# A convolution and a gated product pair on one core: product 2 begins in tile 0 and follows by 60 steps, unit 1 convolved in the ring, new work lists

## The chip, the cores and the metric

The kernel runs on one core of one Trainium2 chip. The metric is the time of one execution in microseconds (us) as the device measures it. Its engines work side by side, each on its own queue of instructions, and wait for each other by semaphores: TensorE (PE, matrix products), VectorE (DVE), ScalarE (ACT), GpSimd (POOL) and SyncE (SP, which here issues transfers). Product results are written to PSUM, which has eight banks of 512 float32 for each of 128 partitions.

## What is computed

The input x has 8 sequences of 4096 positions with 192 channels. A causal convolution with 7 taps mixes positions; its weights are a softmax over the taps, one set for each of 8 heads of 24 channels. The result, as 32768 rows of 192, goes through a product pair with h cos h between.

```python
w = exp(weight - max(weight)); w = w / (sum(w) + 1e-09)        # 8 heads x 7 taps
c[b, s, head, g] = sum_k w[head, k] * x_padded[b, s + k, head, g]
x = c.reshape(32768, 192)
h = x @ w_in                   # 192 -> 2048
g = h * cos(h)
out = g @ w_out                # 2048 -> 192, float32
```

## The kernel before

The rows are cut into 64 tiles of 512 rows (four blocks of 128); two tiles make a unit, so there are 32 units of 1024 rows. All products are taken in bfloat16 and summed in float32.

A unit passes these stations. Its rows are loaded by SP (`load_unit`, 768 KB, and `load_edges`, 96 KB, for the rows before each block). GpSimd casts them to bfloat16 (`cast_unit`). TensorE convolves them with banded matrices in two parts of four heads each (`conv_part`, part 0 named d or c, part 1 named c, lines 191 and 218). ScalarE copies the two banks of a part to `ct` (`conv_out`, line 200). GpSimd doubles `ct` in its free direction (`double_unit`), so that one transfer on SP's queue can transpose it into `cT` (`turn_unit`, line 263) and each column block is there twice, on rows 0 to 63 and 64 to 127. GpSimd mends the first six positions of each block, which need rows of the block before (`mend_edges`). Unit 0 goes another way: its first half is transposed on TensorE (`conv_first`, `turn_first`), its second half is convolved by `conv_rest` with both band halves, doubled while it is copied out, and transposed by a transfer.

A tile then has eight pairs j of column blocks of w_in. `mm1` (line 387, "h0" to "h7") fills two banks with six matmuls. `gcu` (line 399, "s0" to "s7") lets ScalarE take the cosine (a sine with a bias) and VectorE multiply it with h into `g`. `mm2_step` (line 412, "m5" is five steps) makes product 2: 64 steps a tile, two matmuls each, one on the upper and one on the lower 64 rows of the array, so that they run side by side into two banks, `o_ps0` and `o_ps1`. After step 32 the row halves change banks. `Turn` (line 162) guards such a change: an empty instruction on SP's queue waits for the last matmuls of the first half, and the first ones of the second half wait for it. The half-array parts of a convolution use it as well. "q" marks the middle of a tile's product 2 and "p" its end. `evac` copies the two banks out, bank 0 on ScalarE ("P") and bank 1 on VectorE ("Q"), and `store` writes 384 KB. The last tile sums its four blocks in four separate banks, and `finish` copies and stores them one by one.

PSUM holds a ring of three tiles of two banks (`h_pool`) for `mm1` and for convolution parts, and the two banks of product 2. A new ring tile can be written only when the one that had its banks has been read.

The order of work is written out by hand. TensorE's is one list a tile, `PE_ORDER`, with `PE_FIRST` for the first four tiles; ScalarE's and VectorE's follow `ACT_ORDER` and `ACT_FIRST` ("er", "ec1", "ed2" are the copies of convolution parts). The loop at line 480 walks TensorE's list and lets ScalarE's go on as far as its entries have been made. Transfers and GpSimd's work are tied to p and q (lines 526 to 555). Product 2 lags: tile 0 has none of it, and in the steady list a tile of `mm1` begins when the product 2 of two tiles earlier still has 21 steps to go, so 85 steps are left between the two. In tiles 0 and 1 convolutions are made with all 128 rows at once (`whole`), in tile 0 into the banks of product 2 (`o_banks`), which are idle there.

At the start, `band` is filled by sixteen small copies shared out by a string, D for VectorE, P for GpSimd, A for ScalarE (line 318); the first matmuls of the convolution (line 337) need them.

Of the kernel before, what the change touches and what calls it, by code (L numbers as in the profile page):

```python
# [16 lines left out]
def kernel(  # L17
# [72 lines left out]

    def cast_wo(q):
        nc.gpsimd.tensor_copy(out=wo[:, q * HP : (q + 1) * HP], in_=wo_f[:, q * HP : (q + 1) * HP])

# [94 lines left out]

    ct_tiles = {}

    def conv_mm(u, c, ps, i, rows, n0, n1, prev=0, **flags):
# [26 lines left out]
    def conv_part(u, c, banks, whole=False):  # L218


        ps = banks()
        nb = UB + (u == 1)
        sides = [slice(0, 64), slice(64, 128)]

        def mm(i, rows, **flags):
            return conv_mm(u, c, ps, i, sides[rows], 0, nb, **{"start": False, "stop": False, **flags})

        if whole:
            for i in range(4):
                conv_mm(u, c, ps, i, slice(0, 128), 0, nb, start=i % 2 == 0, stop=i % 2 == 1)  # L230
            if u == 2 and c == 0:
                spread_taps(ps[1][:, UB * 2 * G : UB * 2 * G + K])
            yield
        else:
            mm(0, 0, start=True)
            mm(2, 1, start=True)
            turn = Turn()
            turn.mark(mm(1, 0), mm(3, 1))
            yield
            turn.wait(mm(2, 0), mm(0, 1))  # L240
            mm(3, 0, stop=True)
            mm(1, 1, stop=True)
        yield
        if c == 0 and u not in ct_tiles:
            ct_tiles[u] = ct_pool.tile([128, UB + 1, NC, 2, 64], BF16, name="ct")
        for b in range(2):
            conv_out(u, c, ps, 0, 0, nb, nc.scalar.copy, banks=(b,))
            if b and u == 2 and c == 0:
                nc.scalar.copy(tap, ps[1][:, UB * 2 * G : UB * 2 * G + K])
            yield  # L250

    cT = {}

    def double_unit(u):

        ct = ct_tiles[u]
        nb = UB + (u == 1)
# [4 lines left out]

    def turn_unit(u, n0=0, n1=UB + 1):
        ct = ct_tiles.pop(u)
        if u not in cT:
# [17 lines left out]
    def mend_edges(u):  # L283

        if u == 1:
            nc.gpsimd.tensor_copy(out=cT[u][:, 0:UB, :, 0 : K - 1],
# [30 lines left out]
    three = {"D": nc.vector.tensor_copy, "A": nc.scalar.copy, "P": nc.gpsimd.tensor_copy}  # L317
    for i, k in enumerate("DPDPDPADPDPADPAD"):
        q, rows = divmod(i, 4)
# [43 lines left out]
    def conv_rest():  # L363
        banks = o_banks()
        for c in range(2):
            for i in range(4):
                for prev in range(2):
                    conv_mm(0, c, [b[:, 4 * G * 2 * c :] for b in banks], i, slice(0, 128), NB + 1 - prev, UB + 1 - prev, prev,
                            start=c == 0 and prev == 0 and i % 2 == 0, stop=c == 1 and prev == 1 and i % 2 == 1)
        yield  # L370
        for b in range(2):
            for c in range(2):
                conv_out(0, c, [x[:, 4 * G * 2 * c :] for x in banks], NB, NB, UB, copies[1 - b], True, (b,))
        yield
# [3 lines left out]
    turn_first(1)  # L378
    cast_unit(1, 0, NB)
    cast_unit(1, NB)  # L380

# [5 lines left out]
    def mm1(t, j, n0=0, n1=NB):  # L387

        c = cT[t // TPU]
        m0 = (t % TPU) * NB  # L390
# [7 lines left out]

    def gcu(t, j, h, n0=0, n1=NB):
        cs = cos_pool.tile([128, 2, T], BF16, name="cs")  # L400
        part = slice(n0 * 128, n1 * 128)
# [7 lines left out]

    STEPS = 2 * NF  # L410

    def mm2_step(q):
# [13 lines left out]
        else:  # L426

            si, f = divmod(k, NF)
            if half == 0 and f == 0:
                for b in range(2):  # L430
                    o_ps[tt, b, si] = (o_pools[b].tile([128, T], FP32, name="o_ps%d" % b) if si else
                                       ring_banks()[0])[:, 0:D]
            first, last = half == 0 and f == 0, half == 1 and f == NF - 1
        ms = []
        for r in range(2):
# [4 lines left out]
                                       rhs=wo[rows, f // 2, f % 2, :], start=first, stop=last, skip_group_check=True))  # L440
        if i == STEPS - 1:
            turns[tt] = Turn()
            turns[tt].mark(*ms)
        if i == STEPS:
            turns.pop(tt).wait(*ms)

    def evac(t, b):
        if t not in o_sb:
            o_sb[t] = opool.tile([128, NB, D], FP32, name="o_sb")
        copies[b](o_sb[t][:, 2 * b : 2 * b + 2, :].rearrange("p s d -> p (s d)"), o_ps.pop((t, b)))  # L450

# [4 lines left out]
    def finish(t):  # L456
        o_sb[t] = opool.tile([128, NB, D], FP32, name="o_sb")
        for si in range(2):
            for b in range(2):
                copies[b](o_sb[t][:, 2 * b + si, :], o_ps.pop((t, b, si)))  # L460
                store(t, 2 * b + si, 2 * b + si + 1, [nc.scalar, nc.sync][b])

    o_ps, o_sb, turns = {}, {}, {}

    PE_ORDER = "h0 m4 c1 m6 c2 m4 h1 m7 h2 p h3 m13 h4 m10 h5 m6 h6 m3 q h7 m11"
    ACT_ORDER = "s0 ec1 Q ec2 s1 P s2 s3 s4 s5 s6 s7"

    PE_FIRST = ["h0a h0b h1 h2 h3 r h4 h5 d1 d2 h6 h7 c1 c2",
                "p h0 m5 h1 m5 h2 m6 h3 m12 h4 m2 h5 m2 q d1 d2 m5 h6 m6 c1 c2 m3 h7 m3",
                "m5 h0 c1 m10 p c2 h1 h2 m7 h3 m2 h4 m14 h5 m5 h6 m4 q h7 m1",
                "m11 h0 m3 c1 m5 c2 m3 h1 m9 p h2 h3 m10 h4 m9 h5 m8 h6 m5 q h7 m11"]
    ACT_FIRST = ["s0a s0b s1 s2 er s3 s4 s5 ed1 ed2 s6 ec1 ec2 s7", "s0 s1 s2 s3 s4 s5 ed1 ed2 s6 ec1 ec2 s7",
                 "s0 P Q ec1 s1 ec2 s2 s3 s4 s5 s6 s7", ACT_ORDER]

    HALVES = {"": (0, NB), "a": (0, NB // 2), "b": (NB // 2, NB)}
    step = 0
    for t in range(NT + 2):  # L480
        u, second = divmod(t, TPU)
        cu, cc = (u + TPU, second) if t >= TPU else (1 + t, 1)
        conv = {"c": conv_part(cu, cc, ring_banks if t else o_banks, t < TPU) if cu < NU else iter(())}
        if t < TPU:
            conv["d"] = conv_part(cu, 0, ring_banks if t else o_banks, True)
        if t == 0:
            conv["r"] = conv_rest()
        act, done, h = (ACT_ORDER if t >= len(ACT_FIRST) else ACT_FIRST[t]).split(), set(), {}

        def flush():  # L490
            while act:
                k = act[0]
                need = {"P": "p", "Q": "p", "e": "r" if k == "er" else k[1:2] + "2"}.get(k[0], "h" + k[1:])
                if need not in done:
                    return
                act.pop(0)
                if k[0] in "PQ":
                    if 0 <= t - 2 < NT - 1:
                        evac(t - 2, "PQ".index(k[0]))
                elif k[0] == "e":  # L500
                    next(conv[k[1]], None)
                    if k == "er":
                        turn_unit(0, NB, UB)
                        load_unit(2)
                        load_edges(2)
                        cast_wo(0)
                elif k[0] == "s" and t < NT:
                    gcu(t, int(k[1]), h.pop(k[1:]), *HALVES[k[2:]])

        for k in (PE_ORDER if t >= len(PE_FIRST) else PE_FIRST[t]).split():  # L510
            if k[0] == "h" and t < NT:
                h[k[1:]] = mm1(t, int(k[1]), *HALVES[k[2:]])
            elif k[0] in conv:
                next(conv[k[0]], None)
            elif k[0] == "m":
                for q in range(step, step + int(k[1:])):
                    mm2_step(q)
                step += int(k[1:])
            elif k[0] == "p":
                assert step % (2 * STEPS) == 0  # L520
            elif k[0] == "q":
                assert step % (2 * STEPS) == STEPS
            done.add(k)
            flush()

            if k == "q":
                if second == 0 and t and u + 1 < NU:
                    mend_edges(u + 1)
                if t == 1:
                    cast_unit(3)  # L530
                    mend_edges(1)
                if second == 0 and u + 3 < NU:
                    cast_unit(u + 3)
            if k == "p":
                if second == 1 and t > 1 and cu < NU:
                    double_unit(cu)
                if second == 0 and t and u + 1 < NU:
                    turn_unit(u + 1)
                if t == 1:
                    turn_unit(1)  # L540
                if 0 <= t - 2 < NT - 1:
                    store(t - 2)
                if t == NT + 1:
                    finish(NT - 1)
            if k == ("p" if t > 1 else "q") and second == 1 and u + 4 < NU:
                load_unit(u + 4)
                load_edges(u + 4)
        if t == 0:
            double_unit(1)
            cast_wo(1)  # L550
            load_unit(3)
            load_edges(3)
            cast_unit(2)
        if t == 1:
            double_unit(2)

# [29 lines left out]
```

## Time and profile before

| What | Value |
|---|---|
| median of 3 runs | 713.9 us (713.43 to 715.75) |
| profiled execution, first to last instruction | 714.0 us |
| TensorE busy, matmuls | 703.3 us, 11828 |
| VectorE, ScalarE, GpSimd busy | 646.7, 590.4, 300.9 us |
| cosine of a pair (L402, 128x1024) | 1028 ns |
| multiply of a pair (L406, 128x1024) | 1222 ns |
| copy of a convolution bank (L209, 128x384; 128x432) | 483 ns; 548 ns |
| copy with doubling (L343, 128x768) on ScalarE | 799 ns |
| copies out of product 2 (L450) on VectorE, ScalarE | 558 ns, 473 ns |
| first product of a tile begins (L395) | 10.44 us |
| last matmul ends | 710.49 us |

An instruction's mean time is from its start to its end; neighbours on one engine overlap a little, so that multiplies in a row start some 1.14 us apart and cosines 0.92. A line L395 is line 395 of the kernel. "PE" is TensorE at a matmul and "PEld" the load of its weights, which runs beside matmuls. "SPq" stands for SP's queue. An arrow such as "<-DVE g L406" names what ended the idle time before an instruction. A granted clock of 1.00 is full speed of TensorE.

### The profile page before, as it was taken

To read this page: it belongs to the slowest core of one execution; us is meant where nothing else is said; L and a number is where in the kernel's file an instruction comes from. 1 tells how busy PE (TensorE), PEld (TensorE's weight loads), DVE (VectorE), ACT (ScalarE), POOL (GpSimd) and SP (SyncE) were. 2 spreads that over 40 slices of the span, in tenths; PEclk is the share of its full clock that TensorE was granted. 3 is DMA by queue.
4 is the path that set the end of the run, shared out by engine and by line. 5 is a ranking of instruction groups with operands and counts; after the bars stand their busy time and mean duration, and the time that the engine had idled before them with its cause. 6 is when DMAs were issued, how large, how long until landed. Compare 5 with 4: busy or idle time off the path is not lost.

```text
span 714.0 us, 26519 instructions
## 1 busy us (share of the span) xinstructions
PE 703.3 (99%) x11828; PEld 538.3 (75%) x11829; DVE 646.7 (91%) x601; ACT 590.4 (83%) x719; POOL 300.9 (42%) x307
## 2 busy tenths in 40 slices
PE   7899999999999999999999999999999999999997
PEld 3577777777777777777777777777777777777776
DVE  7799999999999999999999999999999999999995
ACT  7788888888888888888888888888888888888774
POOL 6553345553245533445543355534355533453200
PEclk9999999999999999999999999999999999999999
DMA  8954553545644535544546534445535565513402
GB/s 213 232 110 115 145 127 100 138 94 127 146 104 115 142 86 137 146 107 113 126 94 146 144 97 124 113 107 145 137 91 138 98 122 145 122 52 92 95 25 68
DMA packets 183713, 85.25 MB, mean 119 GB/s; under 512 B 111664, under 2 KB 183216, under 8 KB 183600
## 3 DMA queue, kind: packets, MB, share of 16 engines
q1 hardware_dynamic: 182888, 82.59, 48.3%
q8 instruction: 92, 1.51, 0.9%
q0 software_dynamic: 416, 0.79, 0.8%
q14 instruction: 21, 0.17, 0.1%
q10 hardware_dynamic: 296, 0.20, 0.1%
HBM read 31.36 MB, written 25.17 MB: 79 GB/s over the span
## 4 chain that ended last, share of the span: by engine, by line
PE 96%; DVE 1%; DMA 1%; ACT 1%; issue 0%; POOL 0%; POOLq 0%; SPq 0%
PE o_ps L439 47%; PE h L395 46%; PE h L194 3%; DMA cT<-ct 1%; DVE g L406 0%; ACT cs L402 0%; PE h L439 0%; DVE band L320 0%; POOL mask L131 0%; ACT mask L136 0%; ACT ct L343 0%; PE o_ps L194 0%; DVE diag L309 0%; DVE cT L361 0%; PE h L358 0%
## 5 line engine op out<-in xcount | busy, mean ns | idle before, releaser
L406 DVE TENSOR_TENSOR g<-h,cs 128x1024 bf16<-128x1024 f32 (+1 forms) x513 | 606.4, 1220 | 32.3 <-ACT cs L402 21.8
L402 ACT ACTIVATE cs<-h 128x1024 bf16<-128x1024 f32 (+1 forms) x513 | 511.9, 1026 | 102.2 <-PE h L395 68.2
L439 PEld LDWEIGHTS <-g 64*128 64x128 bf16 x8192 | 369.5, 94 | 91.2 <-issue 1.2
L439 PE MATMUL o_ps<-wo,g 64*128 64x192 bf16 x8128 | 434.9, 243 | 0.0
L395 PE MATMUL h<-cT,w 64*128 64x512 bf16 (+1 forms) x3078 | 413.7, 376 | 4.7 <-DVE g L406 2.5
L395 PEld LDWEIGHTS <-w 64*128 64x128 bf16 x3078 | 161.1, 94 | 72.4 <-issue 4.8
L292 POOL TENSOR_TENSOR edge_prod<-cT,tap 128x1008 f32<-128x1008 bf16 x30 | 67.2, 2239 | 347.0 <-DMA cT<-ct 347.0
L183 POOL CAST x_bf<-x_f 128x1728 bf16<-128x1728 f32 (+2 forms) x33 | 80.6, 2444 | 6.7 <-DMA x_f<-in_x_dram 6.7
L209 ACT CAST ct<-h 128x384 bf16<-128x384 f32 x120 | 51.8, 483 | 8.5 <-PE h L194 4.8
L450 DVE COPY o_sb<-o_ps 128x384 f32<-128x384 f32 x63 | 35.2, 558 | 23.6 <-PE o_ps L439 23.2
L258 POOL COPY ct<-ct 128x1536 bf16<-128x1536 bf16 (+1 forms) x31 | 45.6, 1472 | 3.4 <-ACT ct L209 3.4
L194 PE MATMUL h<-x_bf,band 64*128 64x192 bf16 (+1 forms) x472 | 41.0, 243 | 0.0
L297 POOL TENSOR_TENSOR edge_prod<-edge_prod 128x144 f32<-128x144 f32 x60 | 33.3, 554 | 4.7
L295 POOL TENSOR_TENSOR edge_prod<-edge_prod 128x432 f32<-128x432 f32 x30 | 30.3, 1009 | 2.4
L450 ACT COPY o_sb<-o_ps 128x384 f32<-128x384 f32 x63 | 29.8, 473 | 1.6 <-PE o_ps L439 1.6
L194 PEld LDWEIGHTS <-band 64*128 64x128 bf16 (+1 forms) x496 | 24.7, 94 | 2.1 <-issue 1.0
L298 POOL TENSOR_TENSOR cT<-edge_prod 128x144 bf16<-128x144 f32 x30 | 18.3, 608 | 2.4
L260 POOL COPY ct<-x_bf 128x192 bf16<-128x192 bf16 x60 | 19.2, 349 | 0.0
L108 PE MATMUL o_ps<-zero 128*128 128x512 bf16 x12 | 4.7, 554 | 1.3 <-DVE zero L103 1.3
L108 PEld LDWEIGHTS <-zero 128*128 128x128 bf16 x15 | 1.6, 121 | 3.3 <-issue 1.9
L460 DVE COPY o_sb<-h 128x192 f32<-128x192 f32 x1 | 0.4, 358 | 3.7 <-PE h L439 3.7
L460 ACT COPY o_sb<-h 128x192 f32<-128x192 f32 x1 | 0.3, 319 | 3.8 <-PE h L439 3.8
(62 smaller groups left out, 43.3 us busy)
## 6 DMA issues: line engine op xcount, KB each, us to landing
out_dram<-o_sb SPq DMA_DIRECT2D x63, 384.0 KB
x_f<-in_x_dram SPq DMA_DIRECT2D x30, 768.0 KB
x_f<-in_x_dram SPq DMA_DIRECT2D x31, 96.0 KB
x_f<-in_x_dram SPq DMA_DIRECT2D x4, 384.0 KB
wo_f<-in_moe_w_out_dram SPq DMA_DIRECT2D x4, 384.0 KB
w<-in_moe_w_in_dram POOLq DMA_DIRECT2D x2, 384.0 KB, 6.3
cT<-ct SPq DMA_TRANSPOSE x32
out_dram<-o_sb ACTq DMA_DIRECT2D x2, 96.0 KB
```

The costliest lines, as they stand in the source:

```text
L183: copy(out=bf[u][:, n0 + o : n1 + o, :].rearrange("p n (h k r) -> p (n h) k r", k=NC, r=R), in_=x_tiles[u][:, n0:n1, :].rearrange("p n (h ...
L194: return nc.tensor.matmul(out=ps[i // 2][:, 0 : (n1 - n0) * 2 * G].rearrange("p (n k i r) -> p i n k r", n=n1 - n0, k=NC, i=2)[:, i % 2], ...
L209: copy(o[:, :, 0, :], i[:, :, 0, :])
L258: nc.gpsimd.tensor_copy(out=ct[:, 0:nb, :, 1, :], in_=ct[:, 0:nb, :, 0, :])
L292: nc.gpsimd.tensor_tensor(out=edge_prod, in0=window, in1=tap.rearrange("p (a b k) -> p a b k", a=1, b=1).to_broadcast([128, NC * UB, K - 1 ...
L295: nc.gpsimd.tensor_tensor(out=edge_prod[:, :, :, 0:3], in0=edge_prod[:, :, :, 0:3], in1=edge_prod[:, :, :, 3:6], op=ALU.add)
L297: nc.gpsimd.tensor_tensor(out=edge_prod[:, :, :, 0], in0=edge_prod[:, :, :, 0], in1=edge_prod[:, :, :, j], op=ALU.add)
L395: nc.tensor.matmul(out=h[:, i, n0 * 128 : n1 * 128], lhsT=w[rows, k, j, :], rhs=c[rows, m0 + n0 : m0 + n1, k, :], start=(k == 0), stop=(k ...
L402: nc.scalar.activation(out=cs[:, :, part], in_=h[:, :, part], func=AF.Sin, bias=math.pi / 2.0, scale=1.0)
L406: nc.vector.tensor_tensor(out=g_tiles[t][:, 2 * j : 2 * j + 2, part], in0=h[:, :, part], in1=cs[:, :, part], op=ALU.mult)
L439: ms.append(nc.tensor.matmul(out=o_ps[tt, b, si], lhsT=g_tiles[tt][rows, f, s * 128 : (s + 1) * 128], rhs=wo[rows, f // 2, f % 2, :], star ...
L450: copies[b](o_sb[t][:, 2 * b : 2 * b + 2, :].rearrange("p s d -> p (s d)"), o_ps.pop((t, b)))
```

## The change

The lists are written anew, and GpSimd's work and the transfers, which were tied to p and q, become entries of TensorE's list: K casts a unit, L loads one, D doubles, X transposes, Y mends, W casts half of w_out, O stores what is ready; a digit names the unit where it is not that of the steady rule. Twelve steps of product 2 stand in tile 0, and 87 are issued by the end of tile 1 (49 before). In the steady list four steps of the last tile's product precede the next tile, which makes the lag 60. Copies out of product 2 follow p in the same tile. X stands after c2 in even tiles, Y in odd ones.

Unit 1 takes ring banks for its convolution in tile 0, since the two other banks are in use. `conv_rest` gives each half of the heads a bank of its own, and ScalarE copies each in one instruction of 128x768. Three more parts (d1, c1 and those of unit 2) are made with 128 rows as before, under names with the unit's number. In the last tile the two groups of blocks go through fourteen of sixteen column blocks each before the last two of each, each group has its own Turn, and bank 1 of the tile before is copied by ScalarE ("A"). ScalarE gives one of its three band copies to GpSimd. The assertions on `have` check the lists while the program is built and leave no instruction. The core of the diff:

```diff
-    for i, k in enumerate("DPDPDPADPDPADPAD"):
+    for i, k in enumerate("DPDPDPDPDPDPDPAA"):
...
+                    h = 4 * c + i
+                    nc.tensor.matmul(out=banks[c][:, 0 : 2 * D].rearrange("p (n k i r) -> p i n k r", n=NB, k=NC, i=4)[:, i],
+                                     lhsT=band[:, h, 128 * prev : 128 * prev + 128],
...
-        for b in range(2):
-            for c in range(2):
-                conv_out(0, c, [x[:, 4 * G * 2 * c :] for x in banks], NB, NB, UB, copies[1 - b], True, (b,))
+        for c in range(2):
+            nc.scalar.copy(
+                out=ct_tiles[0][:, NB:UB, :, :, 4 * R * c : 4 * R * (c + 1)].rearrange("p n k t w -> p (n k) t w"),
+                in_=banks[c][:, 0 : 2 * D].rearrange("p (m t w) -> p m t w", t=1, w=4 * R).to_broadcast(
+                    [128, NB * NC, 2, 4 * R]))
...
-    cast_unit(1, 0, NB)
-    cast_unit(1, NB)
...
+    LAST_HALF = [(si, f) for f0, f1 in ((0, NF - 2), (NF - 2, NF)) for si in range(2) for f in range(f0, f1)]
...
-            si, f = divmod(k, NF)
+            si, f = divmod(k, NF) if half else LAST_HALF[k]
...
-        if i == STEPS - 1:
-            turns[tt] = Turn()
-            turns[tt].mark(*ms)
-        if i == STEPS:
-            turns.pop(tt).wait(*ms)
+        if tt < NT - 1:
+            if i == STEPS - 1:
+                turns[tt] = Turn()
+                turns[tt].mark(*ms)
+            if i == STEPS:
+                turns.pop(tt).wait(*ms)
+        elif f == NF - 1 and half == 0:
+            turns[tt, si] = Turn()
+            turns[tt, si].mark(*ms)
+        elif f == 0 and half == 1:
+            turns.pop((tt, si)).wait(*ms)
...
-    PE_ORDER = "h0 m4 c1 m6 c2 m4 h1 m7 h2 p h3 m13 h4 m10 h5 m6 h6 m3 q h7 m11"
-    ACT_ORDER = "s0 ec1 Q ec2 s1 P s2 s3 s4 s5 s6 s7"
...
+    PE_ORDER = "m11 h0 m4 h1 m6 h2 m7 q Y K h3 m7 h4 m7 c1 m4 c2 X L m5 h5 m9 p h6 D O h7 m4"
+    ACT_ORDER = "s0 s1 s2 s3 s4 ec1 ec2 Q s5 P s6 s7"
...
+    PE_FIRST = ["K1 h0a h0b W0 h1 h2 h3 r h4 d11 h5 d21 W1 c11 X0 m1 h6 m11 h7 L2 c21 D1",
+                "m6 K2 h0 m1 L3 h1 K3 m13 q h2 m3 h3 m9 h4 m6 h5 m3 X1 c12 m11 p c22 h6 d12 h7 L4 L5 m17 c13 m4 c23 m1 d22 Y1 D2 m1",
+                "h0 m2 h1 m7 q K4 h2 m11 h3 X2 O m8 h4 Y2 m13 p h5 h6 m9 h7 m7",
+                "h0 m8 h1 m8 q h2 m7 h3 m7 O m1 h4 m3 d13 m4 d23 m6 h5 m4 p h6 h7 m4 D3"]
+    ACT_FIRST = ["s0a s0b s1 s2 er s3 s4 ed11 ed21 s5 ec11 s6 ec21 s7",
+                "s0 s1 s2 s3 s4 s5 ec12 ec22 Q P s6 ed12 s7 ed22 ec13 ec23",
+                "s0 s1 s2 s3 Q s4 P s5 s6 s7",
+                "s0 s1 s2 s3 s4 ed13 ed23 Q s5 P s6 s7"]
+
+    PE_LAST = "m10 h0 m3 h1 m13 h2 m2 q h3 m10 h4 m3 h5 m7 h6 m12 p h7 O m7"
+    ACT_LAST = "s0 s1 s2 s3 s4 s5 s6 P A s7"
...
+    for v in (1, 2, 3):
+        for i, part in enumerate("dc"):
+            conv[part, v] = conv_part(v, i, ring_banks, v < 3)
...
+        def of_unit(k, v):
+            if (k, v) == ("K", 1):
+                cast_unit(1, 0, NB)
+                cast_unit(1, NB)
+            elif (k, v) == ("X", 0):
+                turn_unit(0, NB, UB)
+            elif k == "L":
+                load_unit(v)
+                load_edges(v)
+            else:
+                {"K": cast_unit, "D": double_unit, "X": turn_unit, "Y": mend_edges}[k](v)
...
+            else:
+                v = {"D": cu, "X": u + 1, "Y": u + 1, "K": u + 3, "L": u + 4}[k]
+                if t >= 2 * TPU and v < NU and (k in "DLY") == bool(second):
+                    of_unit(k, v)
```

## The prediction

> **What bounds the kernel now.** I read the page's busy shares and slices first, then TensorE's timeline, then windows laid on the clock's steps, then the chain of waits.
>
> ```profile
> span 714.0 us, 26519 instructions
> ...
> PE 703.3 (99%) x11828; PEld 538.3 (75%) x11829; DVE 646.7 (91%) x601; ACT 590.4 (83%) x719; POOL 300.9 (42%) x307
> ...
> PE   7899999999999999999999999999999999999997
> ```
>
> TensorE (PE) is busy in every slice but the first two and the last. In the chain of waits a tile of the long middle repeats after 10.79 us (56.18, 66.97, 77.76), which is work without a gap: 8 first products at 0.647 ("PE h L395 x12" takes 1.29 or 1.30), 64 steps of product 2 at 0.0825 (64 matmuls, two a step, take 2.64) and 0.33 of convolution make 10.79. No list shortens that; only the first 40 us and the last 10 have room. The timeline of TensorE there (start, length, instruction, idle before and who ended it):
>
> ```profile
> 15.83 0.82 PE L395 MATMUL h<-cT,w 64*128 64x512 bf16 x6 [0.18 <-DVE g L406]
> 16.85 0.53 PE L194 MATMUL o_ps<-x_bf,band 128*128 128x216 bf16 x4 [0.20 <-DVE ct L207]
> 18.03 0.82 PE L395 MATMUL h<-cT,w 64*128 64x512 bf16 x6 [0.65 <-DVE g L406]
> ...
> 22.47 1.34 PE L395 MATMUL h<-cT,w 64*128 64x512 bf16 x6 [2.02 <-DMA cT<-ct]
> ...
> 32.25 0.82 PE L395 MATMUL h<-cT,w 64*128 64x512 bf16 x6 [0.41 <-DVE g L406]
> ...
> 35.50 0.81 PE L395 MATMUL h<-cT,w 64*128 64x512 bf16 x6
> ...
> 38.69 0.82 PE L395 MATMUL h<-cT,w 64*128 64x512 bf16 x6 [0.48 <-DVE g L406]
> ```
>
> Tile 0 has no product 2, so TensorE waits for VectorE (DVE) to free ring buffers and then 2.02 us for the transposed second half of unit 0. A first product occupies 0.65 but ends after 0.82, so each idle time is some 0.17 longer in lost work than the row says. After the long wait come six matmuls in 1.34: half speed. Windows (length, PE busy, granted clock, DMA share, GB/s):
>
> ```profile
> 15.81:19.22 3.41, 2.24 (x18) 1.00 1.65 299
> 19.22:22.64 3.42, 1.40 (x12) 1.00 0.68 136
> 22.64:26.05 3.41, 3.41 (x28) 0.50 1.06 317
> ```
>
> A stretch with 2.24 us of work kept the clock; one with 1.40 was followed by 3.41 us at half.
>
> **Part by part.**
>
> *Band copies.* ScalarE (ACT) gives one of its three to GpSimd (POOL): seven there, in a row. They come every 0.29 us, the sixth from 7.593 to 7.837, so a seventh ends at 8.13; the last quarter now ends with VectorE's at 7.895. The matmuls at 8.04 open the way to the first product at 10.44. Cost 0.24, between 0 and 0.3.
>
> *Unit 0's second half.* Before: two ScalarE copies (0.48) and two of VectorE (0.55). After: two of 128x768 on ScalarE alone, 0.80 each (the row of L343 has 799 ns). They begin when the cosine of s2 ends, 14.5, and end at 16.0; the cosine of s3 (1.03) at 16.95, VectorE's multiply (1.22) at 18.2 against 17.97 before. VectorE's saved copies are thus given back to the wait for ScalarE.
>
> *Unit 1 in the ring.* d11 takes the buffer that s2 frees at 15.78, which h5 used to get, so h5 waits for s3: 18.2 instead of 15.83. The built order of buffers gives c11 the one of d11 (copied out by 18.7), h6 that of h4, h7 that of h5. Then: h5 18.2, c11 18.9, h6 19.4; cosine s5 19.1 to 20.1, multiply to 21.4; h7 21.4 to 22.05. ScalarE's eight in a row (s4, two copies, s5, copy, s6, copy, s7) bring the last multiply to 24.4, against 23.43.
>
> *Twelve steps in tile 0, six more ahead of tile 1.* 18 x 0.0825 = 1.5 us go into gaps; they need the first casts of w_out on GpSimd, W0 (17.37 to 18.84 before) and W1, which moves ahead of the doubling: its load lands at 20.95, so it ends at 22.5, where the first step that needs it stands. TensorE reaches tile 1's first h at 22.55 (22.47 before), after 18 steps instead of none. The transpose X0 is issued at 16.2 instead of 16.79 and landed at 22.2, so the 2.02 us wait is covered.
>
> *Tile 1.* From 22.55: 8 h (5.18), 69 steps (5.69), three convolution parts (0.99) make 34.4; with 0.2 of waits for VectorE, 34.6. Before, tile 2's first h starts at 35.50, with 54 steps issued; after, 87, and a part of unit 3 besides. Lead: 0.9 + 33 x 0.0825 (2.7) + 0.33 = 3.9.
>
> *X1* is moved behind unit 0's row-half Turn on SP's queue, so it is issued at about 25.2, not 23.44. Before it took 10.1 to land, with a 768 KB load in flight until 27.8; the steady ones reach GpSimd 6.1 to 7.9 after issue. By the first the mended edge comes at 35.9 and TensorE waits 1.3; by the second at 33.5 or earlier and nothing is lost. I take 0, since the load's share of its time falls from 4.4 us to 2; behind it SP issues only the loads of units 4 and 5, cast in tile 2 and later.
>
> *Tiles 2 and 3.* Before loses 0.65 at 38.69 (0.48 + 0.17); after, I take 0.2.
>
> *The middle.* Work and period are the same. The lag of 60 puts the steps on the eighth pair 28 steps and three h (4.25 us) behind h7; cosine and multiply need 2.5 and wait about 0.7 for their engines: about 1 us of cover. After p, h6 and h7 (1.3 us) cover the copies; before, one h did. c2 now follows c1 after four steps, not six:
>
> ```profile
> 707.57 0.02 SPq L167
> 707.59 0.05 issue
> 707.63 1.49 PE h L439 x32
> ```
>
> In the trace c1's last matmul ends at 58.231, SP's no-op is over at 58.279, and at 707.6 TensorE took the signal 0.042 later: 58.321. Two steps earlier the weight load would stand at 58.300, the matmul at 58.381. The load comes 0.02 late, the matmul 0.06 after it; at 707.63 the two start together. I take 0; the other bound is 58 x 0.02 = 1.2. SP is never held there: X now follows c2.
>
> *X to Y.* The transpose moves from 1.3 to about 6.3 us into the even tile. With 6.1 to 7.9 to GpSimd and 5.3 of mending it is done 17.7 to 19.5 us into the pair of tiles; needed at 22.5. Before, the margin was 7; now at least 3. Cost 0. The doubling queued behind the mending ends 4 us before the next X. Casts, loads and stores keep their number and stand later in the tile; a load lands 4.5 to 4.75 us after its issue (50.83 to 55.58), its cast follows 8 us after it.
>
> *The end.* P and A (0.47 each) precede the last cosine on ScalarE: that multiply ends 3.3 us after p, wanted at 0.65 + 28 x 0.0825 = 2.96. Cost 0.3. The tail from 710.49 (copy, store) stays.
>
> Sum: 3.9 + 0.45 - 0.24 - 0.3 = 3.8: 710.2 against the profile's 714.0.
>
> *The clock.* Between d11 (ended by 16.3) and c11 (18.9), TensorE does one product in 2.6 us. A window of 3.41 that begins between 14.4 and 16 holds 1.25 to 1.6; on the grid of the run before (15.81 to 19.22) it holds 1.5. Nearer to 1.40 than to 2.24: I take the half clock, about 19 to 22.6. At worst that is 1.7 us; part falls into waits for VectorE. By the chain above, with doubled prices, c11 to h7 and the last cosine come 1.2 later: 711.4, or 711.1 with the grid elsewhere, 711.9 with nothing hidden.
>
> The Trainium skill, TensorE: Matmul & The Clock Gate, section "Part 1: The HAM clock gate", has the clock fall after an idle window of about 3.4 us, on a grid that runs freely. The row disagrees on the first: 1.40 us of work was not enough to keep it. By the page tile 0 keeps its clock and the sum is 710.2.
>
> The profiled 714.0 lies 0.1 over the median of 713.9 (713.43 to 715.75), which I take off.
>
> **Rivals.**
> - *Clock kept* (grid elsewhere): 710.1. For it: half of the places of the grid. Against: 1.5 us is near 1.40.
> - *X1 late, or the Turn's 0.02 paid in each tile*: 1.3 or 1.2 on top: 712.6. For it: X1's 10.1 us; against: the load that shared it ends sooner, and matmuls have started with their loads.
> - *Slower: X to Y misses its tile.* Transpose, mending, first product of the next unit is one chain, 3 us of cover where there were 7. It decides as soon as landing takes over 11 us in the middle; then each of 30 units waits: 0.3 us beyond it is 9 us, 720. For it: X1's 10.1 at the start. Against: thirty steady rows at 6.1 to 7.9.
> - *The change does not do what it says* (steps in tile 0 wait for the casts or for g): lead 2.4 instead of 3.9 and the half clock, 712.9.
>
> **How the numbers follow.** Forecast (half clock moved into tile 0) 0.47, own range 710.6 to 712.0; clock kept 0.27; X1 or Turn 0.09; steps that wait 0.06; slower 0.11. Time: the forecast's, 711.3. Low 709.4 is the kept clock without the band copy's 0.24 and 0.45 of the 0.7 of waits that I take in tiles 1 to 3 and at the end; high 713.4 takes in the third and the last but one. No change is 711.8 to 716.0 (0.3%). Faster: 0.27 and three quarters of 0.47, 0.63; same: the rest of it and the two small rivals, 0.26; slower 0.11.
>
> **What would show it.** Right: no idle for the transpose of unit 0; 87 steps before tile 2's first h, at 34.5 to 36; half clock before 22.6; a period of 10.79; first product at 10.7; some 0.3 idle near the last tile's end. Wrong: a period over 10.82 (Turn), first products of the middle that wait for a cT (X to Y), or a first h of tile 2 after 36.5.

## The result and the profile after

| What | Before | After |
|---|---|---|
| median (lowest to highest, 18 executions each) | 713.43 us (712.98 to 715.75) | 711.66 us (711.57 to 712.94) |
| ratio, 95% interval | | 0.9973, 0.9966 to 0.998 |
| profiled execution, first to last instruction | 714.0 us | 711.2 us |

The change saves 1.8 us, a quarter of a per cent. For each execution the time, the span and the mean granted clock are known. The time is 1.65 to 1.8 us more than the span in all of them: 712.94 with 711.2, 711.6 with 709.9, and before 713.25 with 711.5, 715.7 with 714.0. Both kernels have executions with a stretch of 3.41 us at half clock and executions without one, and the mean clock tells them apart. After: five of 18 with it (clock 0.998, 712.75 to 712.94), twelve at 711.57 to 711.68 without, and one at 712.14 whose mean clock of 0.999 shows no such stretch. Before: in the 31 executions that ran beside the first experiments, seven with it (715.17 to 715.57, median 715.45), the others at 713.03 to 714.21 (median 713.32). Both profiled executions have the half clock; both medians do not. So the two spans above compare like with like (2.8 us), but not with the medians.

The page of the changed kernel, span, busy time and TensorE's 40 slices:

```profile
span 711.2 us, 26528 instructions
...
PE 702.2 (99%) x11828; PEld 536.8 (75%) x11829; DVE 637.4 (90%) x598; ACT 599.9 (84%) x719; POOL 303.7 (43%) x308
...
PE   7999999999999999999999999999999999999997
```

Two slices below 9 at the start have become one. TensorE's busy time fell by 1.1 us (both traces have one stretch at half clock, counted as busy); the rest of the 2.8 us is idle time that is gone. The middle is as before, as the chain of waits of the changed kernel shows (start, length, piece): the period is 486.23 - 475.44 = 10.79.

```profile
475.44 1.29 PE h L411 x12
...
486.23 1.29 PE h L411 x12
```

The first 37 us in TensorE's timeline of the changed kernel (mm1 is now line 411, the multiply 423, a convolution part 196, product 2 458):

```profile
16.71 0.53 PE L196 MATMUL h<-x_bf,band 128*128 128x216 bf16 x4 [1.08 <-POOL x_bf L184]
18.31 1.44 PE L411 MATMUL h<-cT,w 64*128 64x512 bf16 x6 [1.07 <-DVE g L423]
...
21.86 1.07 PE L458 MATMUL o_ps<-wo,g 64*128 64x192 bf16 x22
...
23.92 0.81 PE L411 MATMUL h<-cT,w 64*128 64x512 bf16 x6
...
36.23 0.81 PE L411 MATMUL h<-cT,w 64*128 64x512 bf16 x6
```

The 2.02 us of waiting for the transposed half of unit 0 are gone: 22 matmuls of product 2 stand there. Two waits of about 1 us are left there, for a cast and for the buffer of s3. The half clock now falls between them and tile 1, as windows of the same trace show (length, PE busy, granted clock, DMA share, GB/s):

```profile
14.96:18.38 3.42, 1.27 (x12) 1.00 1.10 328
18.38:21.79 3.41, 3.41 (x18) 0.50 1.25 192
21.79:25.20 3.41, 3.41 (x56) 1.00 1.07 296
```

At the end, the chain of waits shows the price of the last cosine:

```profile
701.40 0.02 ACT o_sb L476
701.43 0.35 issue
701.78 0.29 ACT o_sb L476
702.07 0.08 issue
702.15 1.05 ACT cs L419
703.20 0.02 issue
703.23 1.24 DVE g L423
704.46 0.04 issue
704.51 0.34 PE h L458 x4
```

ScalarE copies twice, then takes the cosine, VectorE multiplies, and TensorE starts again at 704.51. The two matmuls before started at 704.13, and the next two would have followed 0.08 later, at 704.21, so 0.3 was waited.

### The profile page after: what moved, and what is told of

Same layout as the page of the kernel before. It is cut to its first block, busy times and chain, and to the rows that moved or that the text cites. A ratio compares the mean times of both kernels' runs of the same rounds, so it can differ in the third digit from the quotient of the medians.

```text
span 711.2 us, 26528 instructions
## 1 busy us (share of the span) xinstructions
PE 702.2 (99%) x11828; PEld 536.8 (75%) x11829; DVE 637.4 (90%) x598; ACT 599.9 (84%) x719; POOL 303.7 (43%) x308
## 4 chain that ended last, share of the span: by engine, by line
PE 97%; DVE 1%; ACT 1%; POOL 0%; issue 0%; POOLq 0%
PE o_ps L458 47%; PE h L411 47%; PE h L196 3%; DVE g L423 0%; ACT cs L419 0%; PE h L458 0%; DVE band L330 0%; ACT ct L386 0%; POOL mask L132 0%; ACT mask L137 0%; ACT ct L353 0%; DVE diag L319 0%; DVE cT L371 0%; PE o_ps L347 0%; PE h L368 0%
## 5 line engine op out<-in xcount | busy, mean ns | idle before, releaser
L423 DVE TENSOR_TENSOR g<-h,cs 128x1024 bf16<-128x1024 f32 (+1 forms) x513 | 599.9, 1216 | 21.3 <-ACT cs L419 18.6
L476 DVE COPY o_sb<-o_ps 128x384 f32<-128x384 f32 x62 | 34.6, 557 | 42.8 <-PE o_ps L458 42.6
L211 ACT CAST ct<-h 128x384 bf16<-128x384 f32 (+1 forms) x124 | 53.7, 484 | 14.0 <-PE h L196 13.4
L196 PE MATMUL h<-x_bf,band 64*128 64x192 bf16 (+2 forms) x480 | 42.4, 244 | 1.1 <-POOL x_bf L184 1.1
L196 PEld LDWEIGHTS <-band 64*128 64x128 bf16 (+1 forms) x480 | 22.9, 94 | 3.0 <-issue 2.1
L93 POOL CAST wo<-wo_f 128x1536 bf16<-128x1536 f32 x2 | 2.9, 1467 | 2.5 <-DMA wo_f<-in_moe_w_out_dram 2.5
L458 PE MATMUL h<-wo,g 64*128 64x192 bf16 x64 | 3.2, 244 | 0.1
```

The costliest lines, as they stand in the source:

```text
L196: return nc.tensor.matmul(out=ps[i // 2][:, 0 : (n1 - n0) * 2 * G].rearrange("p (n k i r) -> p i n k r", n=n1 - n0, k=NC, i=2)[:, i % 2], ...
L211: copy(o[:, :, 0, :], i[:, :, 0, :])
L423: nc.vector.tensor_tensor(out=g_tiles[t][:, 2 * j : 2 * j + 2, part], in0=h[:, :, part], in1=cs[:, :, part], op=ALU.mult)
L458: ms.append(nc.tensor.matmul(out=o_ps[tt, b, si], lhsT=g_tiles[tt][rows, f, s * 128 : (s + 1) * 128], rhs=wo[rows, f // 2, f % 2, :], star ...
L476: (copy or copies[b])(o_sb[t][:, 2 * b : 2 * b + 2, :].rearrange("p s d -> p (s d)"), o_ps.pop((t, b)))
```

## The experiments

Theory: the start sets the gain (steps moved into waits of tile 0, and where the half clock falls), the end takes 0.3 back, and the middle is unchanged. Rivals: the band copies, the Turn or the transfers take part of it back. Each edit is against the changed kernel unless it says otherwise. The kernel before ran beside each group of experiments; with the full clock its medians there were 713.32 to 713.53, so times of different groups compare to some 0.2 us.

### Four matmuls on zeros in the gap of tile 0

```diff
-"K1 h0a h0b W0 h1 h2 h3 r h4 d11 h5 d21 ...
+"K1 h0a h0b W0 h1 h2 h3 r h4 d11 Z h5 d21 ...
+            elif k == "Z":
+                keep_warm(4, o_pools[0].tile([128, T], FP32, name="o_ps0"))
```

> The changed kernel with four matmuls on zeros (0.22 us each) put between d11 and h5 in tile 0, into a bank of product 2 that is idle there. They run from about 17.2 to 18.1 us, inside TensorE's wait for a ring buffer (18.31), so they delay nothing. Theory (the clock falls because the window before 18.4 held 1.27 us of work): no half clock in the profile and 1.0 to 1.3 us less than the changed kernel's 711.6, so 710.3 to 710.6. Rival (the half clock lies under waits for VectorE and costs nothing): 711.6. Second rival (only a window without any work lowers the clock, so something else did): half clock still there, 711.6.

Measured: 711.66 (711.59 to 711.72, seven executions), ratio 0.9972 (0.9961 to 0.9982), all seven with the full clock, span 710.0. The window of 14.96 to 18.38 holds 2.13 us instead of 1.27; the steps of the clock's grid lie elsewhere in this execution (they begin at 13.63 and 17.04), but a window of 3.41 us holds at least 2.12 wherever between 8 and 26 us it starts. The group near 712.9 is gone, but the median stands where it was, since the median of the changed kernel already belonged to executions that keep the clock. So a span must not be set against the median. The span fell from 711.2 to 710.0: the half clock costs 1.2.

### The kernel before, with five such matmuls

```diff
+            keep_warm(5, o_pools[0].tile([128, T], FP32, name="o_ps0"))
```

They stand behind tile 0's last convolution part, where TensorE waits for the transfer.

> The kernel before with five matmuls on zeros behind tile 0's last convolution, inside the 2.02 us wait for the transfer. Theory: the half clock from 22.64 goes and with it 1.3 to 1.7 us: 711.7 to 712.1 against 713.4, so that most of the distance between the two kernels is gone. Rival (clock cost hidden): 713.4.

Measured: 713.53 (713.45 to 713.93, eleven executions), ratio 0.9997 (0.9989 to 1.0006), all with the full clock, span 711.8 where the profile of before had 714.0. The median does not move, for the same reason. In the kernel before, the half clock costs 2.2 between these two profiles, 2.1 between the medians of its two groups (715.45 and 713.32). The timeline without the half clock is the fair partner of the changed kernel's:

```profile
33.37 0.81 PE L395 MATMUL h<-cT,w 64*128 64x512 bf16 x6
...
36.56 0.82 PE L395 MATMUL h<-cT,w 64*128 64x512 bf16 x6 [0.48 <-DVE g L406]
```

Tile 2 begins at 33.37, with 54 steps issued; the 0.48 (0.65 of lost work) is there as well.

### The eighteen early steps put back behind tile 1's first products

```diff
-                ... d11 h5 d21 W1 c11 X0 m1 h6 m11 h7 L2 c21 D1",
-                "m6 K2 h0 m1 L3 h1 K3 m13 q ...
+                ... d11 h5 d21 W1 c11 X0 h6 h7 L2 c21 D1",
+                "K2 h0 m1 L3 h1 K3 m31 q ...
```

> The changed kernel with its 18 early steps of product 2 (twelve in tile 0, six ahead of tile 1's first product) put behind tile 1's second product; all else stays. Theory (they fill time in which TensorE has nothing else): 18 x 0.0825 = 1.5 us more, 713.1. Rival (VectorE sets the pace in tiles 0 and 1 and its wait would only move): 711.6 to 712.0.

Measured: 713.48 (712.58 to 714.06, eleven executions), ratio 0.9991 (0.9981 to 1.0002). Five executions keep the clock, 712.58 to 713.07, against 711.57 to 711.68 with the early steps. So the steps are worth 1.1 us, not the 1.5 of their own length. The profile shows where the rest stays. Like that of the changed kernel it has the half clock, and its step of the grid is nearly the same (18.33 to 21.75). Tile 1's first product:

```profile
23.38 0.82 PE L411 MATMUL h<-cT,w 64*128 64x512 bf16 x6 [0.56 <-ACT ct L211]
```

In the changed kernel it is at 23.92: without the steps tile 1 begins only 0.54 earlier and tile 2 1.08 later (37.32 against 36.23), so some 0.5 of the steps' time was not idle before. The 1.1 is more than half of the whole gain of 1.8, and the largest single part found. Six executions had the half clock.

### Six steps between c1 and c2 again

```diff
-    PE_ORDER = "... h4 m7 c1 m4 c2 X L m5 ..."
+    PE_ORDER = "... h4 m5 c1 m6 c2 X L m5 ..."
```

> The changed kernel with six instead of four steps between the two halves of a convolution part in the steady list. Theory (the guard's round trip over SP is hidden with four steps too): 711.6, the period of 10.79 unchanged. Rival (0.02 us paid in each of 56 tiles): 1.1 us less, 710.5.

Measured: two groups, 711.59 to 712.11 with the full clock and 712.87 to 713.31 with the half clock, six each (median 712.49, ratio 0.9981, 0.9972 to 0.9991); span of the profiled one, which keeps the clock, 710.1. Its lower group is that of the changed kernel. The Turn with four steps costs nothing that can be seen.

### The band copies as before

```diff
-    for i, k in enumerate("DPDPDPDPDPDPDPAA"):
+    for i, k in enumerate("DPDPDPADPDPADPAD"):
```

> The changed kernel with the sixteen band copies shared out as before. Theory: the first product starts at 10.44 instead of 10.60 and all that follows with it: 0.16 us less, 711.5 where the clock is kept. Rival (the wait for VectorE behind it takes it up): first product at 10.44, time 711.6.

Measured: 711.87 (711.62 to 712.96; six of eleven with the full clock at 711.62 to 711.87), ratio 0.9981 (0.9973 to 0.999), span 709.9. The first product starts at 10.44 again instead of 10.60, but the first cosine at 11.20 instead of 11.24, and no time is gained. The weight loads of the first products show why: behind the first of them the next now waits for the transfer of w_in, which none does in the changed kernel, and that takes up most of the 0.16.

```profile
10.66 1.12 PEld L411 LDWEIGHTS <-w 64*128 64x128 bf16 x18 [0.16 <-DMA w<-in_moe_w_in_dram]
```

Its profile keeps the clock, and so gives the timeline that the sum's first branch described:

```profile
18.27 0.82 PE L411 MATMUL h<-cT,w 64*128 64x512 bf16 x6 [1.04 <-DVE g L423]
19.02 0.54 PE L196 MATMUL h<-x_bf,band 128*128 128x216 bf16 x4
...
19.59 0.81 PE L411 MATMUL h<-cT,w 64*128 64x512 bf16 x6
...
21.46 0.82 PE L411 MATMUL h<-cT,w 64*128 64x512 bf16 x6 [0.15 <-DVE g L423]
...
22.60 0.83 PE L411 MATMUL h<-cT,w 64*128 64x512 bf16 x6
...
34.94 0.81 PE L411 MATMUL h<-cT,w 64*128 64x512 bf16 x6
```

These are h5, c11, h6, h7, the first product of tile 1 and that of tile 2: forecast at 18.2, 18.9, 19.4, 21.4, 22.55 and 34.6. It also shows why the clock was kept with the same work list. The stretch of 14.96 to 18.38 holds 1.27 us of work here too, but the steps of the clock's grid lie elsewhere in this execution. The full clock first begins at 6.25 us here and at 4.72 in the profile of the changed kernel. There the half clock begins 13.66 later (18.38), in the kernel before 17.07 later (22.64 after 5.57): four and five steps of 3.41. Counted so from 6.25:

```profile
13.08:16.49 3.41, 2.51 (x32) 1.00 1.11 300
16.49:19.90 3.41, 2.16 (x20) 1.00 1.35 237
```

### Half of unit 0's copy back to VectorE

```diff
-            nc.scalar.copy(
+            copies[c](
```

> The changed kernel with the second copy of unit 0's second half (128x768) given to VectorE, so that both engines copy as before. Theory (the wait of s3 for ScalarE sets h5, and with it tile 0): the cosine of s3 ends 0.7 earlier, but VectorE is busy with its copy (0.96) until 16.7, so the multiply starts at 16.75 instead of 17.03: 0.3 less, 711.3 where the clock is kept. Rival (ScalarE alone is the better choice, since the transfer waits for the later copy): X0 0.5 later, same or up to 0.5 more.

Measured: 711.40 (711.14 to 711.61, six executions), ratio 0.997 (0.9959 to 0.9982), span 709.4, the full clock in all six. ScalarE is free earlier, s3's multiply starts at 16.46 instead of 17.03, and h5 and the first product of tile 1 follow:

```profile
17.73 0.82 PE L411 MATMUL h<-cT,w 64*128 64x512 bf16 x6 [0.56 <-DVE g L423]
...
22.09 0.83 PE L411 MATMUL h<-cT,w 64*128 64x512 bf16 x6
```

So the second of the two copies on ScalarE costs 0.5 us between the profiles (tile 1 at 22.60 and 22.09, spans of 709.9 and 709.4). Between the medians of executions with the full clock it is 0.2 (711.62 and 711.40), no more than the groups differ, so the size is not settled. The same kernel taken again, to see the clock:

> The changed kernel with the second 128x768 copy on VectorE and nothing else, taken again: six runs had the full clock throughout, where the changed kernel loses it in 6 of 18. Theory: the gap between d11 and h5 is 0.6 us shorter with this copy, but a badly placed step of the grid still holds less than 1.7 us of work, so that one run in six or more lies near 712.5, the others at 711.1 to 711.6. Rival: the shorter gap is enough to keep the clock wherever the grid falls, and no run is above 711.9.

Measured: 711.39 (711.13 to 712.02, six executions), ratio 0.997 (0.9958 to 0.9981), again the full clock in all six. (The changed kernel lost it in five of 18, not six.) The rival held for the clock. Slid over its records, a window of 3.41 us holds at least 1.74 us of TensorE's work wherever between 8 and 26 us it starts; in the changed kernel at least 1.26. The run at 712.02 has the full clock; what moves such executions is seen in the last two experiments.

### The transpose later in the tile

```diff
-    PE_ORDER = "... c2 X L m5 h5 m9 p h6 D O h7 m4"
+    PE_ORDER = "... c2 L m5 h5 m9 p h6 D O h7 X m4"
```

> The changed kernel with the steady transposes issued behind the last product of the even tile instead of behind c2, some 3.7 us later. It tests the rival that was slower. In the changed kernel's trace a mending ends 2.3 us ahead of the next unit's first product where the transfer takes 7.9 us to GpSimd, and about 4 us where it takes 6.1. Theory (a cliff): the long ones are 1.4 us late, in about half of 28 units: 20 us more, 720 to 735. Rival (enough cover left, or the transfer is quicker there): 711.6.

Measured: 734.58 (733.58 to 735.6, four executions), ratio 1.029 (1.0274 to 1.0306). The slower rival is real, only not reached by the change. Its view of waits (us in all, times, longest) and, below it, TensorE's timeline at one unit:

```profile
PE h L411 <- POOL cT L308: 15.1, 16, 1.6
```

```profile
325.47 0.82 PE L411 MATMUL h<-cT,w 64*128 64x512 bf16 x6 [0.73 <-POOL cT L308]
```

The transpose is issued at 312.40, GpSimd's mending begins at 320.13 and ends at 325.4, and the next unit's product waits for it. In the changed kernel the same chain runs from 300.65 over 308.57 to 313.85, with the next unit wanted at 315.94: the cover is 2.1 us.

Not all of the 22.9 us that are lost is this wait. The late transpose also holds up SP's queue, and with it the empty instruction of Turn for which the middle of product 2 waits. The view of waits and the chain of waits:

```profile
PEld L458 <- SPq L168: 7.8, 14, 0.8
```

```profile
290.32 5.39 SPq L275
295.82 0.75 PE o_ps L458 x14
```

How the loss divides between the two was not measured.

### Three of the edits together, and two matmuls on zeros

The edits of the first, fifth and sixth experiment in one kernel.

> The changed kernel with the four matmuls on zeros, the band copies shared out as before and the copies of unit 0's second half on both engines. Theory (they add up): 0.16 + 0.3 less than 711.6 and no half clock, 711.2 in nearly every execution. Rival (one of the two earlier starts is taken up by the transfer or by VectorE): 711.5 to 711.7.

Measured: 711.42 (711.36 to 711.54, six executions), ratio 0.997 (0.9959 to 0.9982), span 709.7, the full clock in all. The four matmuls on zeros hold h5 up until 18.02, with no idle time before it, where the copy alone gave 17.73. Two of them, with the copy on VectorE and the band copies of the changed kernel:

> The changed kernel with the second 128x768 copy on VectorE and two matmuls on zeros between d11 and h5 in tile 0 (extra work of 0.43 us at full speed; no part of the computation). In the run with four of them they held h5 up, 18.02 against 17.73 with the copy alone. Theory: two end before s3's banks come free at about 17.7, h5 stands at 17.73, the clock is kept in every execution, span 709.4, time 711.1 to 711.4 (709.4 + 1.7). Rival: the copy alone sets the time and two matmuls are too few to fill a badly placed step of the clock's grid: some executions lose the clock and stand 1.0 to 1.3 above the others.

Measured: 711.55 (711.17 to 712.16, eight executions), ratio 0.9965 (0.9952 to 0.9977), span 710.1. The full clock is kept in all eight and h5 stands at 17.72, as the theory had it, yet four of eight lie at 711.8 to 712.2. The timeline of the profiled one of those names what is late next, the cast of the second half of w_out:

```profile
22.52 0.34 PE L458 MATMUL o_ps<-wo,g 64*128 64x192 bf16 x4 [0.45 <-POOL wo L93]
```

### Two steps moved behind tile 1's first product

```diff
-                "m6 K2 h0 m1 L3 h1 ...
+                "m4 K2 h0 m3 L3 h1 ...
```

Together with the copy on VectorE.

> The changed kernel with the second 128x768 copy on VectorE, and in tile 1 four steps of product 2 instead of six ahead of the first product, and three instead of one behind it. Theory: in the three runs with this copy the start of tile 2 follows the end of GpSimd's cast of the second part of w_out (21.88, 22.13 and 22.47 us; first cosine of tile 2 at 32.46, 32.72 and 33.06), because the last two of the six steps need it, and it moves with the landing of that load. Two steps later it is over before they come, whatever the landing: first cosine of tile 2 at 32.3 to 32.5, span 709.3 to 709.5, time 711.0 to 711.2 with no run above 711.5. Rival: the transfer that brings unit 0's second half, or another thing that moves with the loads, ends just as late and moves with them: the runs spread over 711.1 to 712.1 as before.

Measured: 711.24 (711.1 to 711.97, seven executions), ratio 0.997 (0.9958 to 0.9981), the full clock in all. Five lie at 711.10 to 711.31, two at 711.89 and 711.97. The rival won: without the steps that need w_out, the product waits instead for the transposed half of unit 0:

```profile
22.65 0.82 PE L411 MATMUL h<-cT,w 64*128 64x512 bf16 x6 [0.58 <-DMA cT<-ct]
```

The profiled execution is one of the two late ones. The transposed half has landed at 22.5 in it, at 22.3 in the profile with two matmuls on zeros and at 21.7 in that of the copy alone, where the cast of w_out began at 21.22, 21.00 and 20.41: the two move together. (The cosine that the text above gives at 32.46, 32.72 and 33.06 is the last one of tile 1; tile 2's first stands 2.8 later, at 35.28, 35.53 and 35.87. They move alike.)

This was the lowest median of all, 0.4 below the changed kernel; the intervals of their ratios overlap. Its surer gain is that no execution lost the clock in it or in the kernels with the same copy (19 executions without matmuls on zeros).

## Why the prediction came out as it did

The time (711.3 for 711.66), the sign and the range were right. That the time came so close is in part luck: two errors largely cancel, the half clock (1.2 too much) and a span set against a time (1.8 too little).

- **The chance of the half clock: wrong.** "I take the half clock" was the likeliest case, with the kept clock as a rival at 0.27. The half clock occurs as described (window of 1.27 us of work, then 3.41 at half, tile 1 at 23.92 where 22.55 + 1.2 was forecast), but in five of 18 executions, so the median keeps the clock. The text itself had the count: starts between 14.4 and 16 are 1.6 of a grid of 3.41, less than half of the places, and a median needs more than half. In three of the kernels with this gap unchanged (the changed one, band and Turn) it was 16 of 41; where the gap was filled or shortened, by matmuls on zeros or by the copy on VectorE, it was none of 40. By limits of 1.40 (clock lost) and 1.74 (the least that a window holds in the kernels with the copy on VectorE, which kept it in 19 of 19), in the changed kernel's trace starts over 1.0 to 1.7 us of the grid lose it, 0.3 to 0.5: an estimate from these traces that fits the 16 of 41.
- **"The profiled 714.0 lies 0.1 over the median of 713.9, which I take off": wrong.** A span was set against a time, which is 1.7 more, and an execution with the half clock against a median without. With both put right, the sums stand as 710.2 + 1.7 = 711.9 (clock kept) and 711.4 + 1.7 = 713.1. The first is the one to compare with 711.66.
- **The sum in spans: right to 0.3.** 710.2 forecast and 709.9 to 710.0 measured with the clock kept, 711.4 and 711.1 to 711.2 with the half clock. The clock's 1.2 measured 1.2. Inside the sum small misses cancel: from 714.0 the measured terms are 3.6 for the lead, with the band copies in it, 0.65 and -0.3, 3.95 for the 3.8.
- **Lead at tile 2: 3.9 forecast, 3.6 measured** (tile 2 at 34.94, not 34.6; 35.50 - 34.94 + 2.7 + 0.33). The term at fault is "three convolution parts (0.99)". From tile 1's first product to tile 2's (22.60 to 34.94 with the clock kept) pass 12.33; less 5.18 and 5.69, that leaves 1.46 for the three parts, the two tiny matmuls that prepare the tap weights and the changes between them. TensorE has no idle time in tile 1, for the 0.2 of waits.
- **Waits in tiles 2 and 3: better than taken.** The 0.65 at the third pair of tile 2 is gone and no new one came, for the 0.2 forecast. Which edit removed it was not tested.
- **Band copies: 0.24 forecast, none measured.** The first product did move (10.60, not 10.44), so the mechanism is right; the price is hidden, most of it under the transfer of w_in.
- **er on ScalarE alone: right in size, and one wait missed.** s3's multiply starts at 17.03 and h5 at 18.27 to 18.31 (18.2 forecast). d11 stood at 16.71, not 15.8, behind GpSimd's cast of unit 1, unseen in the prediction; it costs nothing, since h5 waits for s3 in any case. That it "gives back" VectorE's copies is borne out by undoing half of it: s3's multiply starts at 16.46.
- **W1 and the transpose X0: right.** The transpose was issued at 16.05 to 16.09 (16.2 forecast); tile 1 began at 22.60 with the clock kept. The second cast was over at 22.1, not 22.5, "where the first step that needs it stands"; once the chain ahead was shortened, this was the wait.
- **X1: right.** Issued at 25.41 with the clock kept (25.2 forecast), landed in 6.3 us after an issue at 26.71, not in 10.1. The rival of 1.3 did not occur.
- **Turn: right,** 0, shown by undoing it. **End: right,** 0.30 of waiting for 0.3.
- **X to Y: right in sign, the cover overstated.** "At least 3" was 2.1. The transpose is issued 6.3 after the even tile's first product, as forecast, but the next unit is needed 21.6 after that product (two periods), not 22.5, which is right only when counted from the eleven steps ahead of it. GpSimd started 6.0 to 7.9 us after issue, as the steady rows before had it. The late transpose showed the cliff.
- **The change doing less than it says:** excluded, since the 18 steps are issued before tile 1 and are worth 1.1.

The accounting without the half clock, both sides kept: tile 2 at 33.37 before with 54 steps, at 34.94 after with 87 and a part more: 33 x 0.0825 + 0.33 - 1.57 = 1.48; the 0.65 at tile 2's third pair; 0.3 back at the end. That is 1.8, the difference of the spans 711.8 and 710.0 and of the medians.

## What to carry to other kernels

Where executions fall in groups, ask first to which group the profiled one and the median belong, and compare spans with spans; a state met in fewer than half of the executions moves the highest time, not the median. In a start-up that waits for several loads, filling a wait by moved work is worth it up to the next late load only: here the gain stopped at w_out and then at the transpose, which came late together. A price that the trace shows is paid only if nothing later hides it: the band copies' 0.16 was plain in the first product's start and cost nothing.

## What the runs showed of the hardware that was not expected

The clock can be lost by a step of its grid that is far from idle: 1.26 us of 3.41 with work (early steps undone), 1.27 (changed kernel) and 1.40 (before) were each followed by 3.41 us at half clock, whereas 1.98 (two matmuls on zeros), 2.02 (two steps moved) and 2.16 (band copies) kept it. Of the five profiles in which the gap of tile 0 is unchanged, three have a step of the grid with 1.26 or 1.27 and lose the clock (changed kernel, early steps undone, late transpose); two have none there under 2.16 and keep it (band copies, six steps between c1 and c2). The grid starts at a different time in each execution (first full clock at 4.68 to 7.93 us over thirteen profiles), which makes one kernel's times fall in two groups 1.25 us apart, or 2.1 in the kernel before.

The Trainium skill, TensorE: Matmul & The Clock Gate, section "Part 1: The HAM clock gate", says that the grid runs freely, and these profiles agree. It has the clock fall after an idle window; if that means a window without work, the rows above disagree, at 37% to 41% of a window busy.

The loads of the first 21 us land up to 0.8 us apart in executions of nearly the same list: the cast of w_out's second half began at 20.41, 20.66, 21.00 and 21.22 in four profiles with the copy on VectorE, the first cosine of tile 2 followed at 35.28, 35.53, 35.87 and 36.00, and the spans were 709.4, 709.7, 710.1 and 710.2. This is the spread that remains with the full clock.
